# FNet mixing gated by a GLU on one Trainium2 core: a new order table, new page homes, and a first small fetch on ScalarE's queue

## The chip, the cores and the metric

The kernel runs on one core of one Trainium2 chip. The metric is the device time of one execution in microseconds (us), lower being better; the times given are medians over runs. Five engines work side by side, each through its own instructions in the order in which they were issued: TensorE (PE: matmuls; PEld: the loading of their weights), VectorE (DVE), ScalarE (ACT), GpSimd (POOL) and SyncE (SP, which here only issues transfers). Engines wait for each other through semaphores.

## The reference

```python
xn = layernorm(x)                          # x: 2048 x 512
a, b = xn @ dft_hid_re.T, xn @ dft_hid_im.T
s = dft_seq_re @ a - dft_seq_im @ b        # 2048 x 2048 matrices
h = sigmoid(xn @ w_gate) * (xn @ w_up)     # 512 -> 1792
out = x + s * silu(h @ w_down)             # 1792 -> 512
```

All data are float32.

## The kernel before

Matmuls run on pairs of reduced-precision numbers: an operand is split into a high part (`hi`, made by ACT) and the remainder (`lo`, made by DVE), and three matmuls hi·hi, hi·lo, lo·hi are added up (`split`, `mm3`, lines 373 to 380). Large products are cut into 2 x 2 blocks and done with seven block products instead of eight, so DVE also forms sums and differences of blocks ahead of the splits and behind the products.

The work falls into stages. First a head: x is loaded, normalised, transposed by matmuls against an identity matrix, and the first chunks of the gate and up products are taken while matmuls of a tile of ones (`gb`, `ub` from `ones`) keep PE busy. Then seven groups of 256 of the 1792 inner columns, for each half of the sequence: gate and up products from the weights `w_gu`, sigmoid and product, and the down product from `w_down`. Its partial results are added into `g_part` in DRAM by accumulating transfers that POOL issues. The statistics of later rows go through a small DRAM tensor `m_part` and come back broadcast over all partitions; the loaded transposed x (`in_x_t`) is normalised with them by DVE. After that come the sequence transform (blocks of `c_re`, `c_im` loaded, summed by DVE, split; an inner operand kept in `i_part`; sums of xn in `s_part`; results put to `f_part`) and the transform along the hidden axis (`w_h`, `w_part`), with the output added into `out`.

Data live in 54 buffers of the same size in SBUF, called pages (128 partitions x 1024 words, 512 KB); nearly every transfer moves one page. Each new page takes its buffer from the string `HOMES` (lines 270 to 282), letter by letter, so that a letter that comes again is a buffer used again, and the new user waits until the old one's readers are done.

No instruction is issued where the Python code calls it. All calls on the five engines are recorded in a list (`Queue`, `Recorder`, lines 306 to 321), and `emit` (line 324) then issues them by number as the table `ORDER` (lines 33 to 271) lists them. That is why nearly every row of the profile has line 331. The table thus sets the order on each engine and in each queue, and which instruction stands beside which. Lists of due times in the code (such as `LATE3`, `XN`, `CSUM`, lines 645 to 663 and 1040) only set the order of recording.

Loads are issued by SP (`nc.sync.dma_start`), stores and accumulations by POOL (`nc.gpsimd.dma_start`), and a single output piece at the end by ACT. Each queue issues in order: an instruction that waits for its page holds back those behind it.

Of the kernel before, what the change touches and what calls it, by code (L numbers as in the profile page):

```python
# [9 lines left out]
F32 = mybir.dt.float32  # L10
# [5 lines left out]
P = 128  # L16
# [17 lines left out]
1 15 20 0 3 2 4 16 72 5 31 21 7 19 6 22 9 29 11 32 13 23 73 17 8 74 24 10 26 176 25 12 108 27 30 33 50 28  # L34
36-38 211 39 34 40 14 49 51 41 52 48 42 71 43-44 53 70 18 35 55 54 80 56 45 47 46 64 79 65 62 57 63 66 60 81
67-69 59 75-77 82 78 89 84-85 83 86-87 90 88 91 61 92 58 109 96 110 93 101 402 94 97 102 105 98-99 95 100
117-118 113 119-120 103 111-112 104 125-126 154 123 121 124 127 122 128-129 135 130 143 139-140 144-146 106
150 178 151 141 133 155 142 152 114 153 220 230 156 115 157 147-148 443 162 134 163 116 158-159 136 160 164
161 137 180 168-169 177 172-173 206 170 179 138 171 174 201 175 185 165 186 181 191 166 192 149 187-189 218
190 167 203 193-194 212 195-196 182 197 107 198 183 207 204 208 205 199 131 200 221 219 132 222 213 202 214  # L40
231 209-210 223-224 253 242 215-216 225-226 238 217 232 239 227-228 246 243 235 247-248 263 249-250 266 229
236 267 240 284 348 241 285-286 245 233 256-257 287 244 288 254 237 255 258-260 264 261 234 268-269 265
270-271 489 272 251 273-275 293-294 262 276-277 289-290 278 252 279 303 282 304 280-281 361 291 283 292 295
302 296 381 297-298 312-313 301 299 324 300 316-317 320 309 423 321 305 307 306 325 314 340 315 318 310 319
322 362 323 663 330 311 331 349-352 341 444 353 326 354 445 328 344 329 469 332 363 333 470 334-335 327 336
403 337 355-357 345 358 346 359-360 365-366 541 364 367-371 347 377 372-374 379 375-376 442 383-384 378 385
438 386 382 387-389 380 395 390-392 446 393-394 397 424-425 396 426 308 427 399 428 420 429 338 398 436 339
405 404 406 460 407-408 342 409-410 467 411-413 421 414-415 447 416 430-433 417 434-435 439 471 419 472 418
473-474 400 475-476 448 422 483 449-451 437 452-453 440 454 461 455-456 401 464 462 457-459 441 477 465 478
463 479-482 619 491 466 492-493 484 494-495 485 496 343 529-531 545 503 497-498 542 499 468 500-501 487 505  # L50
502 532 535 533 486 534 504 515-516 666 517-518 488 519 536 520 506 552 507 537 553-554 510 590 555-557 580
521-522 527 523-525 511 526 558-561 581 564 562 490 582 563 546 538 547-548 565 549 539 550 592 512 551
566-568 528 569 513 583 570 540 571-572 593-594 575 595-597 573 598 577 599 696 514 600-602 574 603-604 606
584 605 705 608 668 609 543 610 631-632 576 633-634 544 635 607 636 648 585 591 643 649 588 586 650 664 645
614 508 646 184 587 647 625 611 620 612-613 637 578 651 638 621 639 589 615 640-641 669 652 642 616 654-655
617 656-657 653 627 658-659 644 670 626 671 622 661 672-673 660 674-675 618 629 676 662 677-679 682 680 630
681 686 683 687-689 692 684 690-691 685 726 509 693 727 697 728 698 694 729-730 709 731-732 712 623 713 695
628 714-715 733 716 624 717 710 718 699 719 724 700 720-722 707 701 711 723 735-737 970 738 667 665 739-741
706 757 703 758 742 759 773 760 747 761 743 725 762-764 777 765 734 751 708 769 752-754 744 755-756 969 750
797-799 745 771 789 749 790-791 795 792 746 793-794 774 766 815 767 781 768 783 775 778 784-785 770 704 786  # L60
772 787 779 788 748 809-811 776 803 800-802 782 796 806-807 804 808 829 812 830 850 805 831-832 816 780
833-834 823-824 813 825 859 826 821 827 814 828 846 840-841 835 842 817 837 860 838-839 862-863 971 864 836
865 847 866 844 818 848 867-868 843 869 935 870 874 871 845 822 872-873 878 875 879 849 880 930 881 884 882
876 883 887 931 885 888 851 819 889 886 890 893 891 897 892 906 857 852 907 877 908 853 909-910 855 858
911-912 894 913-914 932 915 898 916 978 899 917 904 923 968 924 900 925 856 920 896 921-922 967 936 918 926
937-939 927 919 940-941 929 928 972 951 861 980 952 965 953 948 973 955 949-950 934 902 942 975 954 943-944
905 1093 945 981 946 895 947 956-957 901 999 979 958-959 976 962 960-961 987 966 1022 988-990 977 991-992
963 933 1001-1002 985 1003 1054 1004-1005 982 1006-1007 993-995 1000 996 986 997 1008 998 1010 1026 1011
1009 1012 1021 1013-1014 983 964 1015 1023 1028-1030 1016 1031-1032 984 1033 1017 1034-1035 1024 1036-1037
1027 1040 1038-1039 1042 1041 1043-1044 1052 1045 579 1046-1047 1118 820 1057 1048 1018 1025 1058 854 1059  # L70
1049 1060 1119 1061 702 1053 1062 1073-1074 1157 1050 1075-1076 1079 1077-1078 1063 1080 1064-1066 1055
1067-1068 1082-1083 1069 1084-1085 1070 1086 1071 1087-1088 1096 1158 1097 1089 1098 1072 1099-1100 1165
1090 1056 1101 1111-1113 1108-1109 1122 1110 1124-1126 1120 1127-1128 1094 1129-1130 1136 1131-1133 1115
1121 1134-1135 1114 1102 1095 1103 1116 1104 1081 1105 1091 1106-1107 903 1166 1156 1141-1143 1217 1147-1148
1137 1149 1138 1117 1153 1139-1140 1167 1123 1144 1168-1170 1145 1171-1172 1092 1146 1150-1152 1173 1154
1174-1176 1179 1019 1177-1178 1202-1204 1159 1205 1164 1206-1207 1160 1184-1186 1193 1181 1188 1182 1161
1183 1196 1180 1197 1051 1198 1194 1199-1201 1231 1190 1187 1232-1233 1191 1234 1020 1219 1189 1235-1236
1211-1212 1155 1213 1192 1255 1215 1256-1258 1223 1259 1162 1260 1208 1195 1209 1250 1210 1225 1214 1220
1226-1227 1252 1228 1221 1216 1229-1230 1224 1240-1242 1237 1244 1238 1222 1239 1261 1243 1262-1264 1267
1251 1265-1266 1246 1272 1248 1273 1268 1274 1269 1279 1270-1271 1289 1280 1275 1290-1292 1253 1247  # L80
1293-1294 1283-1284 1276 1285 1278 1286 1218 1287-1288 1299 1277 1296 1300 1249 1301-1302 1281 1305 1303
1245 1304 1319 1295 1254 1320-1321 1311 1322-1324 1297 1313 1306 1314-1315 1282 1307 1316-1317 1298 1318
1325-1326 1312 1327-1328 1331 1329-1330 1354 1334 1355-1356 1338 1335 1357-1359 1308 1340 1332 1341-1342
1423 1343-1345 1360 1346 1163 1352 1347 1361 1348-1349 1339 1350 1363 1362 1351 1387-1389 1353 1333
1379-1381 1366 1382 974 1383-1384 1367 1390 1386 1391-1392 1369 1373 1397 1374-1375 1336 1376 1364 1377-1378
1368 1435 1385 1436-1437 1337 1438 1454 1439 1365 1440 1394 1456 1408-1409 1371 1410 1399 1411-1413 1393
1429 1372 1430 1425 1431 1395 1432-1434 1310 1414 1427 1415-1416 1402-1403 1400 1426 1404-1407 1420 1417
1398 1418 1309 1419 1515 1459-1461 1396 1462 1370 1463 1421 1464 1401 1441 1422 1471 1442-1445 1455 1446
1465 1448 1466 1428 1467-1468 1447 1469-1470 1473 1451 1472 1474-1478 2059 1485 1480 1486 1452 1487-1488
1457 1489-1492 1479 1458 1493-1494 1450 1495 1481 1496-1497 1501 1516 1502 1511 1449 1503 1517-1519 1499  # L90
1520 1482 1521-1522 1498 1484 1504-1505 1538 1506 1523 1507 1524 1483 1525-1527 1453 1528-1529 1566 1530
1508 1531 1500 1542 1509 1543 1597 1544 1513 1545-1546 1540 1547-1548 1541 1549 1554 1550-1552 1567 1553
1565 1556 1539 1557 1571 1558 1602 1532-1535 1559-1560 1596 1536 1561 1573-1574 1563 1555 1537 1575-1576
1562 1577 1568 1578 1590 1564 1585 1591 1514 1592 1579 1594 1580-1582 1604 1512 1583-1584 1587-1589 1510
1608 1593 1609 1569 1610-1611 1424 1595 1612 1603 1613 1633 1600 1634-1636 2060 1637 1586 1638 1620 1572
1631 2061 1621-1624 1598 1629 1625 1570 1639-1640 1601 1641 1626 1642-1644 1627 1614 1658 1615 1606
# [238 lines left out]
def fnet_glu_kernel(ctx: ExitStack, tc: tile.TileContext, x, x_t, c_re, c_im, w_h, w_gu, w_down, out):  # L335
# [1218 lines left out]
```

## Time and profile before

| | |
|---|---|
| median of 3 runs | 802.28 us (800.14 to 802.34) |
| the profiled execution's own time | 807.1 us |
| its span, first to last instruction | 805.3 us |
| mean granted TensorE clock | 0.999 |
| PE busy | 786.8 us (98%), 3488 matmuls |
| DVE busy | 735.6 us (91%) |
| ACT busy | 546.6 us (68%) |
| POOL busy | 132.5 us (16%) |
| moved by transfers | 190.98 MB, 237 GB/s over the span |

Busy time is the union of an engine's instructions. A busy PE need not be a PE at full rate, so the number of matmuls in a stretch says more than its busy time. In the rows of a timeline, the brackets at the end give how long the engine was idle just before, and what it waited for by the profile's inference. A row on SPq or POOLq is the issue of a transfer.

### The profile page before, as it was taken

How to read it: one execution, taken by the hardware profiler on the slowest of the kernel's cores; microseconds unless marked ns; L12 is line 12 of the kernel's file. 1: busy time of each engine (PE TensorE's matmuls, PEld its weight loads, DVE VectorE, ACT ScalarE, POOL GpSimd, SP SyncE). 2: the span in 40 equal slices, each digit the busy share in tenths (PEclk: the TensorE clock that was granted, in tenths of full speed). 3: DMA queues.
4: the chain of work that ended last, by engine and by line, in shares of the span. 5: the costliest groups of instructions: out<-in, count | busy, mean ns of one | idle time of the engine just before them, and what ended most of it. 6: DMA issues, size and time to landing. Idle time of an engine off the chain costs nothing.

```text
span 805.3 us, 10034 instructions
## 1 busy us (share of the span) xinstructions
PE 786.8 (98%) x3488; PEld 642.9 (80%) x3488; DVE 735.6 (91%) x893; ACT 546.6 (68%) x800; POOL 132.5 (16%) x181
## 2 busy tenths in 40 slices
PE   8999999898999999999999999999999999999997
PEld 7888788686788888888888877778778888888885
DVE  8999997788987979899999987899999999999984
ACT  6778999577776878877887944655475264649450
POOL 3004452121122222311201100100100100001031
PEclk9999999999999999999999999999999999999999
DMA  9403999887679999999987899968995986888066
GB/s 343 128 27 131 231 219 208 203 170 157 146 163 282 251 256 277 285 285 214 258 290 273 192 293 320 270 195 316 384 384 199 393 317 224 328 351 313 1 97 112
DMA packets 54786, 190.98 MB, mean 237 GB/s; under 512 B 6096, under 2 KB 6352, under 8 KB 54736
## 3 DMA queue, kind: packets, MB, share of 16 engines
q0 software_dynamic: 21168, 73.42, 41.0%
q1 hardware_dynamic: 33488, 116.87, 39.9%
q8 instruction: 27, 0.44, 0.2%
q14 instruction: 23, 0.19, 0.1%
q10 hardware_dynamic: 80, 0.07, 0.0%
HBM read 120.06 MB, written 73.94 MB: 241 GB/s over the span
## 4 chain that ended last, share of the span: by engine, by line
PE 74%; DMA 11%; issue 6%; DVE 5%; ACT 1%; POOL 1%; SPq 0%; DVEq 0%; ACTq 0%; POOLq 0%
PE pd L331 16%; PE ga L331 11%; PE ua L331 10%; PE gb L331 9%; PE ub L331 9%; PE uc L331 9%; PE gc L331 9%; DVE page L331 5%; DMA g_part<-page 3%; DMA f_part<-page 2%; DMA page<-in_c_re_dram 2%; DMA page<-i_part 2%; DMA page<-in_w_gu_dram 1%; ACT page L331 1%; DMA page<-in_c_im_dram 1%
## 5 line engine op out<-in xcount | busy, mean ns | idle before, releaser
L331 DVE TENSOR_TENSOR page<-page 128x1024 f32<-128x1024 f32 (+5 forms) x712 | 646.6, 970 | 35.3 <-ACT page L331 17.2
L331 ACT ACTIVATE page<-page 128x1024 fp32r<-128x1024 f32 (+4 forms) x392 | 350.6, 935 | 133.5 <-DVE page L331 89.0
L331 PE MATMUL pd<-page 128*128 128x512 f32 x708 | 185.0, 392 | 5.1 <-ACT page L331 3.9
L331 PEld LDWEIGHTS pd<-page 128*128 128x128 f32 x708 | 131.6, 188 | 37.2 <-ACT page L331 8.4
L331 PE MATMUL ga<-page 128*128 128x512 f32 (+1 forms) x558 | 142.0, 387 | 0.5 <-DVE page L331 0.5
L331 PE MATMUL ua<-page 128*128 128x512 f32 (+1 forms) x546 | 140.1, 388 | 1.1 <-DVE page L331 0.6
L331 POOL DMA_DIRECT2D g_part<-page x84 | 70.7, 893 | 322.9 <-ACT page L331 304.8
L331 PEld LDWEIGHTS ga<-page 128*128 128x128 f32 x558 | 103.9, 188 | 22.8 <-issue 0.9
L331 PEld LDWEIGHTS ua<-page 128*128 128x128 f32 x546 | 101.6, 188 | 23.8 <-DVE page L331 2.0
L331 ACT ACTIVATE page<-pd 128x512 f32<-128x512 f32 (+2 forms) x165 | 91.4, 576 | 36.0 <-PE pd L331 30.9
L331 PE MATMUL gc<-page 128*128 128x512 f32 (+1 forms) x420 | 108.7, 384 | 0.3 <-DVE page L331 0.3
L331 PE MATMUL uc<-page 128*128 128x512 f32 (+1 forms) x420 | 107.8, 384 | 0.3 <-DVE page L331 0.3
L331 PE MATMUL gb<-page 128*128 128x512 f32 (+1 forms) x420 | 104.6, 382 | 0.5 <-ACT gb L331 0.5
L331 PE MATMUL ub<-page 128*128 128x512 f32 (+1 forms) x384 | 99.2, 387 | 2.1 <-ACT ub L331 1.8
L331 PEld LDWEIGHTS gc<-page 128*128 128x128 f32 x420 | 77.5, 188 | 17.1 <-DVE page L331 1.6
L331 PEld LDWEIGHTS uc<-page 128*128 128x128 f32 x420 | 77.8, 188 | 16.5 <-DVE page L331 1.0
L331 PEld LDWEIGHTS gb<-page 128*128 128x128 f32 x420 | 76.5, 188 | 17.0 <-ACT gb L331 1.2
L331 PEld LDWEIGHTS ub<-page 128*128 128x128 f32 x384 | 71.4, 188 | 18.0 <-ACT ub L331 2.9
L331 ACT ACTIVATE page<-ga 128x512 f32<-128x512 f32 x48 | 28.6, 597 | 13.5 <-PE ga L331 12.0
L331 POOL DMA_DIRECT2D f_part<-page x16 | 8.7, 543 | 168.0 <-DVE page L331 142.0
L331 DVE TENSOR_TENSOR page<-page,gc 128x512 f32<-128x512 f32 x34 | 23.2, 683 | 8.8 <-PE gc L331 6.6
L331 ACT ACTIVATE page<-ua 128x512 f32<-128x512 f32 x34 | 20.4, 599 | 12.9 <-PE ua L331 11.2
(62 smaller groups left out, 256.4 us busy)
## 6 DMA issues: line engine op xcount, KB each, us to landing
g_part<-page POOLq DMA_DIRECT2D x84, 512.0 KB, 7.5
page<-in_c_re_dram SPq DMA_DIRECT2D x64, 512.0 KB, 6.1
page<-in_c_im_dram SPq DMA_DIRECT2D x33, 512.0 KB, 6.3
page<-i_part SPq DMA_DIRECT2D x28, 512.0 KB, 6.1
page<-in_w_gu_dram SPq DMA_DIRECT2D x24, 512.0 KB, 6.7
f_part<-page POOLq DMA_DIRECT2D x16, 512.0 KB, 6.8
page<-f_part SPq DMA_DIRECT2D x16, 512.0 KB, 6.2
i_part<-page POOLq DMA_DIRECT2D x14, 512.0 KB, 7.5
```

The source lines that it names most:

```text
L331: f(*map(found, a), **{n: found(v) for n, v in k.items()})
```

## The change

The instructions are those of before but for one. The table `ORDER` and the string `HOMES` are replaced by others, made with longer transfers assumed; and right after the identity matrix, ACT's queue fetches 32 words of the first two weight tiles into a tile `touch` that nothing reads. All lines of the code behind the table stand a little further down, so that the recorded instructions show line 332 in place of 331.

```diff
 ORDER = """
-1 15 20 0 3 2 4 16 72 5 31 21 7 19 6 22 9 29 11 32 13 23 73 17 8 74 24 10 26 176 25 12 108 27 30 33 50 28
+1 15 20 0 3 2 16 72 5 31 4 21 7 19 6 22 9 32 11 29 13 176 17 53 74 8 23 33 10 73 24 26 25 108 36 27 30 28
...
 HOMES = (
-    "abcdefghijklmnopqrstuvwxyzABCDEFGHIJKLMNOPQRSTUVWXYZ01ospduyBAFrGJCDTwq1xMdPegAISKNXUvBxDELhqPdxtBwK"
+    "abcdefghijklmnopqrstuvwxyzABCDEFGHIJKLMNOPQRSTUVWXYZ01nupdvCBzFqAJGDTsrY1fMQxezSvPLNIwKXTEhsYy1tTDPS"
...
     ident = const.tile([P, P], F32, name="ident")
     make_identity(tc.nc, ident)
+    touch = const.tile([P // 8, 2], F32, name="touch")
+    tc.nc.scalar.dma_start(touch, w_gu[0, :, :: 8, 0, :1].rearrange("k p o -> p (k o)"))
     ones = const.tile([P, 512], F32R, name="ones")
```

What the tables do is seen in the rows of the engines. The number behind a name is the buffer's, given out in the order of issue, so that the same data bear other numbers in the two kernels.

Place 1 is SP's queue where the second half of the sequence is normalised (between the 530th and the 720th matmul of the program). The rows are loads; `m_part` holds the statistics, `in_x_t` the transposed x that they normalise. Before:

```order
L331 DMA page_1270<-in_x_t_dram 128x1024
L331 DMA page_1283<-in_w_gu_dram 128x1024
L331 DMA page_1380<-in_x_t_dram 128x1024
L331 DMA page_1388<-in_x_t_dram 128x1024
L331 DMA page_1489<-m_part_80 128x1024
L331 DMA page_1542<-m_part_80 128x1024
L331 DMA page_1579<-in_w_gu_dram 128x1024
```

And in the changed kernel:

```order
L332 DMA page_1296<-m_part_82 128x1024
L332 DMA page_1305<-in_x_t_dram 128x1024
L332 DMA page_1353<-in_w_gu_dram 128x1024
L332 DMA page_1360<-in_x_t_dram 128x1024
L332 DMA page_1371<-in_w_gu_dram 128x1024
L332 DMA page_1553<-in_w_gu_dram 128x1024
L332 DMA page_1576<-in_x_t_dram 128x1024
L332 DMA page_1613<-m_part_82 128x1024
```

The first `m_part` load now stands ahead of the three `in_x_t` loads instead of behind them, and the two no longer follow each other. In the table, 23 matmuls stood between the first of them (page_1489) and the DVE instruction that waits for it; now 99 do (page_1296). For the second it was 75 (page_1542), and is 31 (page_1613).

Place 2 is SP's queue in the sequence transform, around the 2170th matmul. The rows are loads of the transform's blocks (`in_c_re`, `in_c_im`) and of the kept inner operand (`i_part`). Before:

```order
L331 DMA page_4584<-in_c_im_dram 128x1024
L331 DMA page_4589<-in_c_re_dram 128x1024
L331 DMA page_4617<-in_c_re_dram 128x1024
L331 DMA page_4625<-in_c_re_dram 128x1024
L331 DMA page_4639<-i_part_91 128x1024
L331 DMA page_4646<-in_c_re_dram 128x1024
```

And in the changed kernel:

```order
L332 DMA page_4632<-in_c_im_dram 128x1024
L332 DMA page_4636<-in_c_re_dram 128x1024
L332 DMA page_4661<-in_c_re_dram 128x1024
L332 DMA page_4674<-i_part_93 128x1024
L332 DMA page_4684<-in_c_re_dram 128x1024
```

Four loads in a row had 18, 21, 18 and 17 matmuls up to the instruction that waits for them (page_4617, 4625, 4639, 4646); the corresponding four now have 23, 19, 18 and 16 (page_4636, 4661, 4674, 4684). Here the order has changed and the distance has not.

Place 3 is POOL's queue around the 840th matmul, where partial results are added into the four `g_part` tensors of the first half; an addition into a tensor waits until the one before it into the same tensor has landed. Before:

```order
L331 DMA g_part2_83<-page_1748 128x1024
L331 DMA g_part0_81<-page_1724 128x1024
L331 TENSOR_SCALAR shifts_79<-moments_77 128x1
L331 DMA g_part3_84<-page_1811 128x1024
L331 DMA g_part1_82<-page_1854 128x1024
L331 DMA g_part2_83<-page_1911 128x1024
```

And in the changed kernel:

```order
L332 DMA g_part1_84<-page_1861 128x1024
L332 DMA g_part2_85<-page_1738 128x1024
L332 DMA g_part3_86<-page_1885 128x1024
L332 DMA g_part2_85<-page_1926 128x1024
L332 DMA g_part0_83<-page_2000 128x1024
```

Between the two additions into the same tensor (`g_part2`) there stood 84 matmuls in the table; now there are 23.

Over the whole program behind the first 80 matmuls, the median number of matmuls between a load of SP and the first instruction of PE, ACT or DVE that waits for it goes from 43 to 52 (204 loads each). Loads with fewer than 27 matmuls go from 43 to 23: from 3 to 0 between the 560th and the 900th matmul, and from 27 to 15 between the 1870th and the 2570th.

More of the change, by code (lines that the diff above doesn't have):

```diff
@@ L264 @@
[L264 to L267 removed]
+1 15 20 0 3 2 16 72 5 31 4 21 7 19 6 22 9 32 11 29 13 176 17 53 74 8 23 33 10 73 24 26 25 108 36 27 30 28
+211 50 37-40 34 12 48 14 51 18 49 41 52 42-43 71 44-45 80 35 70 57 79 64 47 65 54 101 56 62 102 63 81 55 66
@@ new lines @@
+1057 1049 1058 1054 1059-1060 1048 1061 986 1062 1055 1050 1076-1078 1073 1217 974 1074-1075 1063 1079
+1064-1066 1080 1067-1069 1085-1086 1070 1087 1082-1083 1072 1084 1096 1071 1088 1097-1099 1089 1056
+1100-1101 1223 1111-1113 1108-1110 1124 1114 1125-1126 1052 1127 1094 1128-1129 1157 1130 1136 1131 1115
+1132-1133 1423 1051 1134-1135 1141 1091 1142 1090 1143 1095 1120 1150-1152 1156 1102-1103 1053 1116
+1104-1105 1165 1106 1121 1107 1167 1117 1168 1145 1169 1081 1170 1193 1171 1122 1172 1147 1137 1148-1149
@@ new lines @@
+1286-1287 1224 1288 1272 1295 1273-1274 1269 1253 1249 1270-1271 1289 1248 1290 1276 1291-1292 1275
+1293-1294 1297 1302-1304 1299 1306 1300-1301 1254 1313 1296 1314 1277 1315 1311 1316-1317 1281 1318 1328
+1305 1329 1298 1330 1307 1319-1320 1312 1321-1324 1245 1334 1325 1282 1326-1327 1308 1354-1356 1278
+1357-1360 1340-1341 1163 1335 1342 1361 1343-1344 1218 1345 1390 1352 1391 1331 1392 1346 1332 1347-1348
+1363 1349 1333 1350-1351 1387 1353 1388-1389 1338 1379 1366 1380-1382 1369 1383-1384 1373 1367 1386
@@ new lines @@
+1374-1376 1393 1368 1377-1378 1454 1435 1364 1436 1336 1385 1437 1399 1438 1397 1439-1440 1337 1429-1430
+1339 1394 1431-1433 1425 1395 1434 1402 1365 1403 1398 1404 1427 1405-1407 1459 1371 1455 1460-1462 1396
+1463 1400 1464 1310 1414-1418 1456 1419 1408 1309 1421 1409 1372 1410-1411 1420 1412-1413 1515 1422 1444
+1426 1445-1446 1441 1370 1362 1448 1442-1443 1401 1465 1447 1466-1468 1471 1449 1469 1597 1470 1482
+1473-1474 1516 1457 1475 1485-1487 1472 1488 1483 1489-1490 1428 1476-1478 1491 1480 1492 1451 1493-1494
@@ new lines @@
+1479 1495-1497 1501 1566 1502 1498 1503 1540 1517 1424 1452 1518-1520 1450 1521-1522 1499 1523 1538
+1524-1525 1453 1526 1507 1527-1528 1458 1504-1506 1542 1508 1481 1543 1539 1544-1545 1511 1500 1546-1547
+1532 1484 1533 1513 1534 1529-1531 1509 1554 1548-1549 1535 1550 1512 1551 1565 1552-1553 1556 1536 1557
+1541 1558 2060 1559 1537 1560-1561 1510 1573 1563 1574 1555 1575-1576 1562 1577 2059 1578 1564 1590-1591
+1567 1592 1568 1587 1571 1588-1589 1514 1579-1580 1593 1581-1582 1604 1583 1713 1584 1608-1609 1714 1594
@@ new lines @@
+1707-1708 1848 1701 1709 1717 1847 1718 2233 1703 1719 2231 1720 1711 1721 2234 1722 1660 1723 1738
+1724-1726 1686 1727 2232 1728-1729 2235 1730 1687 1731-1732 1735 1733-1734 1757 1736 1758 1818 1759 1754
+1737 1739 1755-1756 2096 1746 1702 1747 1761 1748-1749 2098 1750 1760 1751 2099 1784 1819 1712 1785 1762
+1786 1767 2030 1822 1768 2064 1769 1753 1770-1772 1821 1740 2097 1741 2065 1742 2100 1743-1745 1788 1773
+1820 1752 1774-1775 2196 1776 2062 1777 1763 1778 2063 1812 1939 1813 2066 1814 1764 1781-1783 1765 1803
@@ new lines @@
+1910 2034 2016 1967 2017-2018 2052 2022 2053-2054 2004 1985 2024 2005-2006 2002 2007-2008 1995 2009 2049
+2056 2050 2003 2051 2263 2037-2038 2265 2039 2035 2040 1997 2041 1911 2042 2090 1986 2091 2036 2092 2405
+2043 2055 2044-2045 2331 2475 2046 2094 2047-2048 2103 2087 2473 2088-2089 2204 2010 2093 2011 2474
+2012-2013 2136 2161 2095 2014 2476 2015 2079 2162 2080 2068 2332 2194 2081-2082 1998 2083-2084 2070 2073
+2086 2074-2075 2104 2076 2403 2077 2058 2078 2404 2111 2069 2298 2112 2057 2296 2113-2114 2067 2268
@@ new lines @@
+2115-2116 2477 2264 2121 2118 2122-2124 2120 2127 2125-2126 2144 2085 2406 2269 2145 2367 2146 2128 2407
+2147-2148 2368 2101 2149 2187-2188 2137 2369 2189 2184 2191 2185-2186 2105 2071 2102 2106-2107 2239
+2108-2109 2190 2110 2195 2205 2225 2299 2117 2226 2192 2227 2266 2222 2206 2223-2224 2138-2139 2376 2207
+2140-2143 2176 2119 2159 2177-2179 2370 2160 2180 2168 2181 2208 2072 2209-2210 2229 2211-2212 2228 2213
+2169-2171 2372 2230 2172 2270 2173-2175 2267 2150 2129 2182 2151-2152 2254 2401 2156 2255 2183 2256 2214
@@ new lines @@
+2438 2215 2260 2373 2216-2217 2135 2193 2218-2219 2371 2333 2153-2154 2201 2536 2155 2257 2220 2258 2202
+2259 2248-2249 2297 2237 2250 2203 2300 2251-2253 2304 2240 2307-2309 2238 2310 2335 2311-2312 2261
+2274-2275 2271 2157 2276 2262 2277-2279 2158 2289 2340 2290-2291 2241 2286 2293 2287-2288 2242 2292 2243
+2236 2244-2245 2221 2294 2246-2247 2272 2313-2316 2302 2317 2273 2318 2324 2320 2325-2326 2321 2436 2328
+2322 2334 2323 2402 2348 2327 2349 2437 2350-2351 2305 2341 2329 2352-2353 2361-2362 2355 2374 2363 2280
@@ new lines @@
+2449 2710 2455 2397 2500-2501 2479 2434 2502 2497-2499 2398 2462 2456 2480 2457 2504 2458-2460 2503 2461
+2445 2485 2463 2486-2487 2538 2488 2483 2489 2566 2490 2527-2528 2620 2529 2547 2478 2531 2548-2549 2484
+2550 2539 2551-2552 2518-2519 2510 2567 2520-2524 2511 2525-2526 2541 2530 2542-2543 2653 2544 2554 2545
+2534 2546 2508 2491-2494 2553 2495-2496 2509 2558-2560 2555 2562 2556 2537 2557 2512 2561 2513 2683
+2514-2516 2540 2517 2568 2533 2569-2571 2769 2563 2944 2572-2573 2535 2584 2580 2585 2532 2586 2621
@@ new lines @@
+2865-2869 2980 2870 2888 2930 2872 2931-2932 2950 2946 2936 2951-2953 2889 3112 2954-2955 2933-2934 2914
+2935 3039 2956-2958 2937 2959-2960 2915 2961 2938 2924 2963 2982 2925-2927 2939 2884 2928-2929 2916 2989
+2890 2912 2990-2992 2962 2993-2994 2947 2983 2996 2984-2985 2948 2998 2986-2988 2917 3009 2964 2975
+2965-2966 3046 2970 3047 2949 3048-3049 2995 3050-3051 2967 2997 2968 3066 2969 2981 2971 3090 2972
+3002-3003 2940 3004 2976 2999-3001 2942 3067 3010-3012 3053 3013-3014 3126 3123 3015 3040-3042 3005 3043
@@ new lines @@
+3259-3260 3239 3262 3261 3263-3265 3270 3240 3266-3267 3280-3281 3251 3282 3134 3293 3171 3294-3295 3032
+3277 3172 3299 3278-3279 3271 3286 3310 3287 3062 3288 3392 3283-3284 3274 3285 3030 3296-3298 3311 3303
+3306 3312 3348 3313-3316 3215 3300 3320-3321 3483 3323 3322 3301 3338-3340 3317 3302 3318 3336 3319
+3324-3326 3393 3327 3307 3328-3329 3341-3342 3364 3268 3343 3333-3334 3308 3335 3362 3330-3332 3350 3481
+3289 3351-3352 3356 3291 3357-3358 3337 3353-3354 3345 3355 3359 3504 3360 3363 3361 3366-3367 2973
@@ new lines @@
+3449 3478 3523 3489 3450-3451 3494 3462 3495-3496 3482 3491 3479 3492 3604 3493 3490 3500 3480 3501-3502
+3511-3512 3484 3513 3497 3487 3498-3499 3517 3522 3518 3456 3488 3519 3508 3506 3509-3510 3528 3486
+3529-3530 3514 3520 3515-3516 3525 3503 3526-3527 3537 3521 3531 3538 3532-3533 3540-3541 3573 3542 3602
+3546-3548 3648 3534 3507 3535-3536 3543 3558 3544-3545 3552 3549-3551 3685 3560 3553 3561 3603 3562 3566
+3539 3567 3554 3568 3563-3565 3555 3569-3571 3556 3578-3579 3559 3557 3580 3574 3581-3584 3607 3575
@@ new lines @@
+3854 3812 3941 3813-3814 3849-3851 4037 3809-3811 3815-3816 3793 3817 3820 3802 3821-3822 3855 3835 3856
+3844 3857 3823 3803 3824-3825 3897 3859-3864 3898 3865 3869-3871 3866 3845 3924 3867-3868 3829 3967
+3830-3831 3873 3884 3833 3885-3886 3826 3914 3827 4026 3828 3887-3888 3832 3889 3874 3984 3875 3843
+3876-3878 3925 3879 3932 3965 3955 3933-3934 3968 3893-3895 3915 3929-3930 3882 3931 3890-3891 4011 3892
+3935 4055 3936-3938 4002 4203 3939-3940 3881 3942-3944 3883 3899-3901 3945-3946 3969 3947 3902-3904 3908
@@ new lines @@
+4640 4645-4646 4678 4647 4651 4609 4652-4653 4664 4648-4650 4641 4666 4663 4667-4668 4693 4669-4670 4665
+4671 4675-4676 4608 4677 4672 4610 4718 4673-4674 4698-4699 4473 4700 4689 4683 4738 4684-4685 4313
+4686-4687 4682 4688 4709 4695-4697 4704 4722 4760 4705-4706 4777 4701-4703 4694 4711 4900 4712 4802
+4713-4715 4710 4716 4723-4724 4680 4725-4726 4761 4727 4737 4728 5036 4729-4732 4736 4740 4776 4741-4742
+4733-4734 4739 4735 4752 4746-4748 4743 4762 4717 4744-4745 4749 4940 4750 4832 4751 4764 5115 4765-4766
@@ new lines @@
+5032 4963 5478 4970 4975 5219 4976-4977 5148 5084 4978 5038 4979 5035 4980-4981 5070 4982-4983 4974
+4992-4993 5000 4994-4996 5003 4997 5004-5006 4984 5001 4985-4986 5361 5007-5008 5198 5009 4991 5010 5215
+5011-5012 5039-5040 5048 5041-5044 5013 5068 5309 5014-5015 5151 5017-5018 5086 5019 5052 5081 5023-5025
+5053 5079 5054 5071 5055 5020-5022 5029 5059 5045 5060-5061 5033 5026-5028 5072-5073 5082 5074-5077 5087
+5030 5088-5092 5111 5056-5058 5097-5098 4971 5099-5101 5095 5102-5106 5093 5107-5108 5062 5080 5094
```

411 lines of the change are left out of this document (168 added, 243 removed).

## The prediction

> **What bounds the kernel now.** I read the page's head first, then the stretches of the span, the groups and issues of transfers, and then the timeline at the places where matmuls are missing.
>
> ```profile
> span 805.3 us, 10034 instructions
> PE 786.8 (98%) x3488; PEld 642.9 (80%) x3488; DVE 735.6 (91%) x893; ACT 546.6 (68%) x800; POOL 132.5 (16%) x181
> ```
>
> PE is the bound, and the change leaves its 3488 matmuls as they are. What can change is the time in which it gets none. The stretches show that; in each row the first number is the length, the number in brackets behind an engine its instructions:
>
> ```profile
> 80.00:140.00 60.00, 59.88 (x262) 48.66 (x261) 54.19 (x84) 54.81 (x88) 24.20 (x29) 1.00 0.99 220
> 140.00:215.00 75.00, 70.22 (x299) 54.75 (x298) 64.00 (x82) 54.00 (x86) 14.58 (x18) 1.00 0.78 162
> 215.00:300.00 85.00, 84.95 (x374) 69.54 (x373) 71.05 (x115) 64.64 (x116) 21.98 (x32) 1.00 0.92 241
> 300.00:440.00 140.00, 140.00 (x618) 115.28 (x617) 134.34 (x174) 112.42 (x172) 22.70 (x30) 1.00 0.96 268
> 440.00:500.00 60.00, 58.80 (x256) 47.43 (x255) 54.66 (x53) 38.76 (x50) 7.46 (x10) 1.00 0.93 262
> 500.00:600.00 100.00, 96.64 (x418) 77.45 (x417) 93.99 (x88) 57.87 (x69) 8.85 (x13) 1.00 0.89 307
> 600.00:720.00 120.00, 120.00 (x530) 99.01 (x529) 117.26 (x110) 65.62 (x74) 4.83 (x9) 1.00 0.82 312
> ```
>
> In 300:440 PE has no idle time: 140 us / 618 = 0.2265 us a matmul, and 120 / 530 gives the same. At that rate 299 matmuls need 67.7 us, so 140:215 loses 7.3 us. In the same way 500:600 loses 100 - 94.7 = 5.3, 440:500 loses 60 - 58.0 = 2.0, 80:140 loses 0.7 and 215:300 loses 0.3. Together 15.6 us of the 805.3 are lost to waits. That is all that a better order can win behind the head.
>
> Two places carry it: A, 140:215 (7.3 us), and B, 440:600 (7.3 us). What waits at A is in the timeline there:
>
> ```profile
> 140.67 2.13 SPq L331 DMA_DIRECT2D page<-m_part  x2
> ...
> 148.94 11.24 DVE L331 TENSOR_TENSOR page<-page 128x1024 f32<-128x1024 f32 x13 [4.88 <-DMA page<-m_part]
> ...
> 152.73 1.06 ACT L331 ACTIVATE page<-page 128x1024 fp32r<-128x1024 f32 x1 [3.88 <-DVE page L331]
> ...
> 154.32 0.96 PE L331 MATMUL pd<-page 128*128 128x512 f32 x3 [1.16 <-ACT page L331]
> ```
>
> The load of the statistics is issued at 140.67, DVE needs it 4.88 us before it lands, ACT then waits for DVE and PE for ACT: one late transfer passed on through three engines. At B it is the same with another load, its transfer first, from the chain that ended last:
>
> ```profile
> 496.32 6.28 DMA page<-in_c_re_dram
> ```
>
> ```profile
> 502.76 2.00 ACT L331 ACTIVATE page<-page 128x1024 fp32r<-128x1024 f32 x2 [5.64 <-DMA page<-in_c_re_dram]
> ...
> 503.85 3.50 DVE L331 TENSOR_TENSOR page<-page 128x1024 fp32r<-128x1024 f32 x3 [2.49 <-ACT page L331]
> ...
> 504.67 0.58 ACT L331 ACTIVATE ub<-gb 128x512 f32<-128x512 f32 x1
> ...
> 505.30 1.66 PE L331 MATMUL ub<-page 128*128 128x512 f32 x6 [1.58 <-ACT ub L331]
> ```
>
> ACT stands still for 5.64 us until the block has landed, and PE's next sum is started by an ACT copy queued behind it. How long transfers take, in us from issue to landing at the end of each row:
>
> ```profile
> g_part<-page POOLq DMA_DIRECT2D x84, 512.0 KB, 7.5
> page<-in_c_re_dram SPq DMA_DIRECT2D x64, 512.0 KB, 6.1
> page<-i_part SPq DMA_DIRECT2D x28, 512.0 KB, 6.1
> page<-m_part SPq DMA_DIRECT2D x3, 512.0 KB, 8.2
> ```
>
> A load takes 6.1 us, as long as 27 matmuls (27 x 0.2265 = 6.12).
>
> **The change part by part.** The sum is made on the profiled execution: span 805.3 us, own time 807.1.
>
> *Place A.* The first statistics load had 23 matmuls (5.2 us) up to the DVE instruction that waits for it, against a landing of 8.2; it now has 99 (22.4 us), and the second 31 (7.0 us). Loads with a lead under 27 matmuls fall from 3 to none there. So this wait goes, and with it DVE's late start, which feeds ACT and PE. What is late next is POOL: two additions into g_part2 now stand 23 matmuls apart (5.2 us), and the second has to wait for the first, 7.5 us by the row above. That is 2.3 us in which POOL holds what is queued behind it, the additions into g_part0 and g_part2 and with them the pages that ACT writes next. The longest such wait so far:
>
> ```profile
> POOL g_part L331 <- DMA g_part<-page: 10.6, 2, 6.1
> ```
>
> So it costs PE between nothing (the next user of that page has room) and 6.1 us; I take the 2.3. The second statistics load, 7.0 against 8.2, may keep DVE waiting 1.2 us; DVE is idle for 11 of the 75 us there, which covers it. Place A: 7.3 - 2.3 = 5.0 us won; bounds 1.2 and 7.3.
>
> *Place B.* Short leads fall from 27 to 15 of the loads there. I let the loss shrink in that proportion: 7.3 x 15/27 = 4.1 us stay, 3.2 us are won. It is not less because the worst run of loads is not eased: around the 2170th matmul four loads in a row have 23, 19, 18 and 16 matmuls where 18, 21, 18 and 17 stood, 3.6 to 5.2 us against 6.1. DVE has no room to take up such delays: in both tables 78 instructions on a whole page and 10 on half a page stand between the 2140th and the 2570th matmul, by the groups and the timeline
>
> ```profile
> L331 DVE TENSOR_TENSOR page<-page,gc 128x512 f32<-128x512 f32 x34 | 23.2, 683 | 8.8 <-PE gc L331 6.6
> ```
>
> ```profile
> 569.33 6.90 DVE L331 TENSOR_TENSOR page<-page 128x1024 f32<-128x1024 f32 x6
> ```
>
> 78 x 1.15 + 10 x 0.68 = 96.5 of the 97.4 us that 430 matmuls take. Whatever DVE waits there beyond 0.9 us, PE waits. Bounds: nothing won, and all 7.3.
>
> *Elsewhere behind the head* 1.0 us is lost (0.7 and 0.3). The median lead of a load grows from 43 to 52 matmuls, 2.0 us more; I take half, 0.5 won, between 0 and 1.0. The transfers in 215:440 hide behind PE now; what it costs if that ends is the second rival.
>
> *The small fetch* is issued by ACT ahead of the sigmoid table's load. An issue on ACT's queue took 0.57 us at the end of this execution:
>
> ```profile
> 800.46 0.57 ACTq L331 DMA_DIRECT2D out_dram<-page  x1
> ```
>
> The start of the kernel, from the timeline:
>
> ```profile
> 0.73 1.35 SPq L331 DMA_DIRECT2D page<-in_x_dram  x3
> ...
> 2.02 0.20 ACT L331 ACTIVATE warm<-mhalf 128x1 f32<-128x1 f32 x1
> 2.12 0.43 SPq L331 DMA_DIRECT2D page<-in_w_gu_dram  x1
> ...
> 3.53 0.69 DVE L331 BATCH_NORM_STATS2 stats<-page 128x6 f32<-128x512 f32 x1 [2.09 <-DMA page<-in_x_dram]
> ...
> 6.18 0.69 DVE L331 BATCH_NORM_STATS2 stats<-page 128x6 f32<-128x512 f32 x1 [0.41 <-DMA page<-in_x_dram]
> ...
> 6.52 0.66 ACT L331 ACTIVATE page<-pd 128x256 fp32r<-128x256 f32 x2 [4.30 <-PE pd L331]
> ...
> 7.38 0.66 PE L331 MATMUL pd<-ident,page 128*128 128x128 f32 x4 [0.66 <-DVE page L331]
> ...
> 8.13 0.63 ACT L331 ACTIVATE page<-page 128x512 fp32r<-128x512 f32 x1 [0.95 <-DMA page<-in_w_gu_dram]
> ...
> 9.09 0.50 PE L331 MATMUL ua<-page 128*128 128x256 f32 x2 [0.46 <-ACT page L331]
> ```
>
> ACT is idle from 2.22 to 6.52, so the issue is covered. The first weights take from 2.12 to 8.1, 6.0 us, the first x only 0.73 to 3.5, 2.8 us; a fetch of words from the same tensor ahead of them may shorten the first access. But even if they came 3.2 us earlier, the transposes of the second x tile end at 8.04, and its copy and the split of the weights still follow on ACT. Only DVE's 0.41 us of waiting for x would go. I take 0.3 us won; at worst the words hold x up by the 3.2 us that the weights are slower, which would be lost in full. The tail is the same twelve half-width matmuls and four DVE steps in both, so nothing is won there.
>
> *Sum:* 5.0 + 3.2 + 0.5 + 0.3 = 9.0 us. The profiled execution would take 798.1 instead of 807.1. The median of the runs, 802.28, is 4.8 us below the profiled one. If that is a fixed extra, 9.0 carry over whole: 793.3. If it is waits that the other runs do not have, 10.8 of 15.6 are there to win from, and 9.0 x 10.8/15.6 = 6.2 give 796.1. I take 794.5, between them.
>
> **The rivals.**
>
> *The leads do not count (no change, 802.3).* A load's place in SP's queue is not its issue: SP mostly waits until a page is free.
>
> ```profile
> SPq L331 <- DVE page L331: 308.6, 67, 56.0
> ```
>
> If pages come free no earlier than before, the loads go out when they did, the waits stay, and the median stays at 802.3. Against it: the statistics load at A now stands 22.4 us ahead of its user, with its own page given anew. For it: at B, the four loads named above. The DMA page of the Trainium skill (DMA: Bandwidth & Descriptors, Anatomy of one DMA) leads to the same result by another way: its fit for transfers of the software queue, 2.0 us plus bytes / 436e3, makes 3.2 us of a 512 KB page by my estimate, and then leads of 16 matmuls (3.6 us) were enough already and the waits had other causes. The trace disagrees: 7.5 us is the median of 84 such transfers.
>
> *Transfers lengthen as they go out earlier (slower, 806.5).* In 215:440 the transfer engines are 0.92 to 0.96 busy, and PE loses 0.3 us of 225. Loads that go out 2.0 us earlier meet more of POOL's writes. If the writes' landing grows from 7.5 to over 9.5 us, the longer leads are eaten up, A and B keep their loss, and 215:300 begins to wait as 140:215 does: 7.3/75 of 85 us is 8.3, and half of it, since only the additions are late, 4.2. For it: these shares. Against it: the bytes are the same, and 140:215, with the least busy transfers (0.78), loses most, so it was not the load on the engines that made them late there.
>
> **How the numbers follow.** A measurement of this kernel can tell about 0.3%, 2.4 us, from no change. The forecast case, some gain at A and B, runs from 788 (all waits gone: 802.3 - 10.8 = 791.5, or 802.3 - 15.9 = 786.4 if the profiled execution had no extra waits) to 799.9, and I give it 0.68. No change, 799.9 to 804.7: 0.15. Slower: 0.17. The range is 788 to 804.5, with little left out below and most of the slower case above. The chances of faster, same and slower are these three.
>
> **What would show it right or wrong.** Right: in the stretch that holds matmuls 560 to 900 (140:215 before) DVE no longer waits for m_part, and 299 matmuls take about 70 us; at matmul 2170, a wait of ACT, DVE or PE for in_c_re or i_part is still there, 1 to 3 us. POOL's wait for g_part stands near the 866th matmul with 2 to 6 us. The first product starts between 8.7 and 9.1 us. Wrong: A still loses 5 us or more; or g_part's landing is over 9.5 us; or new gaps appear in what was 215:440; or the first product starts after 10 us.

## The result and the profile after

The changed kernel takes 797.9 us (median of 5 runs, 796.5 to 798.3), the kernel before beside it 801.6 (5 runs, 800.1 to 802.3). The ratio is 0.995, with a 95% interval of 0.9935 to 0.9965: faster by 0.5%, 3.7 us. With 12 and 35 runs on another chip it was 0.9947 (0.9926 to 0.9967). Predicted were 794.5, in a range from 788 to 804.5.

The profiled execution of the changed kernel took 796.5 us (span 794.2). First the chain of work that ended last; before, 11% of it was DMA and 6% issue:

```profile
PE 94%; DVE 5%; issue 1%; ACT 0%; DVEq 0%; ACTq 0%
```

Then the windows that the prediction spoke of (busy time and number of instructions of PE, PEld, DVE, ACT, POOL; granted clock; transfer share; GB/s):

```profile
140.00:215.00 75.00, 74.83 (x330) 61.15 (x329) 70.92 (x92) 60.00 (x94) 17.18 (x20) 1.00 0.90 184
...
300.00:440.00 140.00, 139.44 (x611) 113.71 (x611) 128.19 (x157) 108.98 (x162) 22.07 (x27) 1.00 0.93 255
440.00:500.00 60.00, 59.61 (x262) 48.74 (x261) 55.33 (x54) 40.32 (x53) 4.40 (x7) 1.00 0.88 273
500.00:600.00 100.00, 99.78 (x435) 80.74 (x435) 98.65 (x92) 58.34 (x70) 8.03 (x12) 1.00 0.87 298
```

Read the count behind PE's busy time. At 0.2265 us a matmul, place A (140:215) holds 330 matmuls where 299 stood, and loses 75 - 330 x 0.2265 = 0.3 us instead of 7.3. Place B (440:600) holds 697 where 674 stood, and loses 2.1 instead of 7.3. The stretch 300:440 lost nothing and now loses 1.6. With 0.2, 1.0 and 0 in 80:140, 215:300 and 600:720, that is 5.2 us in all where 15.6 were lost.

What is left of the waits for transfers, over the whole run (us in total, times, the longest):

```profile
POOL g_part L332 <- DMA g_part<-page: 9.5, 4, 7.2
...
ACT page L332 <- DMA page<-w_part: 3.3, 1, 3.3
...
ACT page L332 <- DMA page<-in_c_re_dram: 0.9, 1, 0.9
```

DVE's wait for m_part (4.9 us) is gone, ACT's waits for in_c_re (10.1 us over the run, 7.6 of them between 440 and 600) shrank to 0.9, and POOL's waits for its own additions remain. The transfers themselves hardly changed; from issue to landing:

```profile
g_part<-page POOLq DMA_DIRECT2D x84, 512.0 KB, 7.2
page<-in_c_re_dram SPq DMA_DIRECT2D x64, 512.0 KB, 5.5
```

### The profile page after: what moved, and what is told of

Read it like the earlier page. It is cut to its first block, busy times and chain, and to the rows that moved or that the text cites. A ratio compares the mean times of both kernels' runs of the same rounds, so it can differ in the third digit from the quotient of the medians.

```text
span 794.2 us, 10072 instructions
## 1 busy us (share of the span) xinstructions
PE 785.4 (99%) x3488; PEld 643.5 (81%) x3488; DVE 736.1 (93%) x893; ACT 546.5 (69%) x800; POOL 134.4 (17%) x181
## 4 chain that ended last, share of the span: by engine, by line
PE 94%; DVE 5%; issue 1%; ACT 0%; DVEq 0%; ACTq 0%
PE pd L332 20%; PE ga L332 15%; PE ua L332 15%; PE uc L332 11%; PE gc L332 11%; PE ub L332 11%; PE gb L332 10%; DVE page L332 5%; ACT page L332 0%; DVE ones L332 0%; DVEq L332 0%; ACTq L332 0%
## 5 line engine op out<-in xcount | busy, mean ns | idle before, releaser
L332 DVE TENSOR_TENSOR page<-page 128x1024 fp32r<-128x1024 f32 (+5 forms) x712 | 646.5, 970 | 24.8 <-ACT page L332 15.8
L332 DVE TENSOR_TENSOR page<-page,uc 128x512 f32<-128x512 f32 x36 | 24.6, 682 | 11.1 <-ACT page L332 6.1
```

The lines of the kernel that those rows point to most:

```text
L332: f(*map(found, a), **{n: found(v) for n, v in k.items()})
```

## The experiments

The theory: the gain is that of leads. A wait goes when a transfer's page is free, and the transfer issued, early enough to land before its user. The rivals: the new order of the engines' own work; the choice of the homes as such; the small fetch.

### The kernel before, profiled again

> The kernel before, unchanged, profiled a second time. If the 4.8 us by which its profiled execution lay over the median were waits of that one execution, this profile shows a shorter span (about 796 to 801 us) and less than 15.6 us lost behind the head, with the same places named, and the shrunken places tell which waits come and go. If they are a fixed extra of profiling, the span is 805 again with 15 to 16 us lost, 7.3 of them in 140:215 and 7.3 in 440:600.

It took 805.8 us (span 804.1). Its windows and its wait for the statistics:

```profile
140.00:215.00 75.00, 73.21 (x317) 58.38 (x316) 68.05 (x87) 57.34 (x89) 15.30 (x19) 1.00 0.86 177
...
440.00:500.00 60.00, 58.76 (x257) 47.57 (x256) 53.38 (x51) 36.93 (x47) 5.85 (x8) 1.00 0.90 266
500.00:600.00 100.00, 95.32 (x412) 76.28 (x411) 94.20 (x88) 58.54 (x70) 8.87 (x13) 1.00 0.91 308
```

```profile
DVE page L331 <- DMA page<-m_part: 3.8, 2, 3.4
```

The places stay, the sizes do not: A loses 3.2 here and lost 7.3, B loses 8.5 and lost 7.3. By what was expected beforehand this decides nothing: the span of 804.1 and 14.7 us lost in all speak for a fixed extra, A's 3.2 speaks for waits that come and go. More is seen across the kernels. The three profiled executions of this order with its own homes were all long ones: 807.1, 805.8 and, with the small fetch, 806.4, each 4 to 5 us over the median of the same kernel's runs. Six profiled executions in the changed order, those whose homes fit it, lay between 1.4 us under and 2.3 us over their medians, and the order of before with place A mended (next section) 1.0 over. So the extra on which the prediction hesitated is not the same for every kernel; it goes where the waits go. Why a profiled execution of before meets the larger waits each time is not shown.

### Place A alone

```diff
 ORDER = """   (before)
-... 889 886 890 ... 1120 1127-1128 1094 ... 1119 1061 702 1053 ... 1106-1107 903 1166 ...
+... 889 886 702 890 ... 1120 1127 903 1128 1094 ... 1119 1061 1053 ... 1106-1107 1166 ...
```

Number 702 is POOL's write of the first statistics, 903 SP's load of them. In `HOMES`, the letters R and 1 change places from that load on.

> Place A alone, without disturbing other pages: in the kernel before, POOL's write of the first statistics stands some 70 matmuls earlier and SP's load of them 24 entries earlier, and homes R and 1 change names from that load on, so that by the profile of before its page is free at 136.0 us (the load went out at 140.67, when the write had landed), while the one displaced page waits 0.1 us. Theory 1 (the wait for the landing): DVE's wait for m_part, 3.4 to 5.8 us in three profiles, falls to 0 to 1.1; 140:215 loses 0 to 3 us instead of 3.2 to 7.3; the median is 1.5 to 4 us under the kernel before, and the spread of its runs stays, since 500:600 still loses 5 to 7. Rival (the wait only moves: DVE then waits for pages that POOL's additions still read, 2.4 to 4.1 us there before): DVE's or ACT's wait for g_part grows by what m_part's falls, median within 1 us of before.

The ratio to before is 0.996 (0.9939 to 0.998), 798.8 against 801.3 us: 2.4 us for two entries and one exchange of names, where the changed kernel beside it on the same chip has 3.2. The intervals of the two overlap, so that by their times place A alone cannot be told from the whole change. The load went out at 132.9 instead of 140.7 us, by the row of SP's queue, and no wait for m_part is left. That row, and the windows:

```profile
132.88 9.05 SPq L322 DMA_DIRECT2D page<-m_part  x2
```

```profile
140.00:215.00 75.00, 75.00 (x332) 61.87 (x331) 71.75 (x91) 59.66 (x94) 15.62 (x20) 1.00 0.83 175
...
440.00:500.00 60.00, 57.80 (x250) 46.29 (x249) 52.28 (x50) 37.09 (x48) 5.13 (x7) 1.00 0.90 275
500.00:600.00 100.00, 96.66 (x420) 77.92 (x420) 95.97 (x90) 57.52 (x68) 7.98 (x12) 1.00 0.90 310
```

Place A loses nothing, place B its 8.2 us as ever, with ACT waiting for the same loads:

```profile
ACT page L322 <- DMA page<-in_c_re_dram: 10.3, 4, 4.9
```

What held the load in before stands in SP's waits between 110 and 165 us. It was not the page, whose last reader had ended at 138.9 us:

```profile
SPq L331 <- DMA m_part<-moments: 12.4, 1, 12.4
```

SP waited 12.4 us for POOL's write of the statistics, which had gone out at 126.9 us and landed at 140.5. In the changed kernel that write goes out at 107.8 us, and in this run at 108.6. The rows of POOL in before and in the changed kernel:

```profile
126.89 1.70 POOL L331 DMA_DIRECT2D m_part<-moments  x1
```

```profile
107.82 1.09 POOL L332 DMA_DIRECT2D m_part<-moments  x1
```

So place A is mended first of all in POOL's queue, which the lists of SP's loads do not show. Write and load were moved together here, so what each would win alone is not known.

So the late statistics carried all that A lost in the profile: with them early, PE's gaps near 183 and 200 us went too, where the trace of before names ACT and pages held by g_part. DVE's wait for pages that POOL's additions still read did not grow either (5.8 us in before, 1.2 here). That settles A, and since the engines' own order is otherwise that of before, the rival of a new order of their work falls for A. For B no such single load was taken alone; that its gain comes from leads rests on the waits for in_c_re that went, not on an experiment. The times of the runs do not show that gain either, since the kernel that still loses 8.2 us at B in its profile cannot be told from the changed one.

### The order with other homes

Four kernels keep an order and change only `HOMES`; each new page gets a place by a rule: the place free longest, or the one freed last, counted by instructions in the order table, or (the fourth) by times. A fifth was a first try at place A, with 702 and 903 moved and 28 other homes changed to make room.

```diff
-HOMES = ("abcdefghijklmnopqrstuvwxyzABCDEFGHIJKLMNOPQRSTUVWXYZ01nupdvCBzFqAJGDTsrY1f..."   (changed kernel)
+HOMES = ("01ABCDEFGHIJKLMNOPQRSTUVWXLYZSNabcdeBfTgZYhXiaLbeOjaSkQlmnopqrPkDTCrhiVjYgd..."   (freed last)
```

> The order of before, with other page homes: each new page takes the place that has been free longest. That takes away some of the short leads: added over the loads behind the head, what a lead from the page's last reader to the new page's first reader lacks to 32 matmuls is 178 matmuls before and 126 here (49 in the changed kernel). Theory 1 (leads): about (178-126)/(178-49) = 0.4 of the gain of the changed kernel, 1 to 2 us faster than before. Theory 3 (order of the work): no change, within 1 us. If the homes of the changed kernel are what counts: 3 to 4 us faster.

> The order of the changed kernel, each new page in the place that has been free longest: the lack to 32 matmuls is 41 instead of 49, so theory 1 says 0 to 0.5 us faster than the changed kernel (797 to 798 us, ratio to before 0.994 to 0.996); theory 3 says the same time.

> The order of the changed kernel, with other page homes: each new page takes the place that came free last. Leads get short again: what they lack to 32 matmuls adds up to 209 behind the head (178 in before, 49 in the changed kernel); the order of every engine's work stays that of the changed kernel. Theory 1 (leads): the gain is gone, 801 to 806 us, with DVE, ACT or PE waiting for loads in 300:440 (lack 43, 4 there in the changed kernel) and in 500:600 (92, was 32), and little lost in 140:215 (3). Theory 3 (order of the work): the gain stays, 797 to 799 us.

> Place A alone: the kernel before with two entries of its order moved, POOL's write of the first statistics to DRAM (about 40 matmuls earlier) and SP's load of them (its page now free 149 matmuls ahead of its first reader instead of 28), and its page home with 28 later homes shifted by a rank to make room. Theory 1 (the wait for that load is what place A loses): 140:215 loses 0 to 2.5 instead of 7.3, 440:600 loses 7.3 as before, the time is 3 to 5 us under the kernel before. Theory 2 (several loads with short leads each cost their own part of A): only the gaps around 150 to 160 go, 2.5 to 3 us, the ones around 174 to 205 stay. Theory 3 (leads do not count, what counts is the new order of DVE and ACT): 140:215 still loses about 7, time unchanged within 1 us.

| kernel | us | ratio to before |
|---|---|---|
| order of before, free longest by the table | 947.2 | 1.184 (1.178 to 1.190) |
| changed order, free longest by the table | 966.6 | 1.205 (1.202 to 1.209) |
| changed order, freed last by the table | 1226.8 | 1.529 (1.525 to 1.534) |
| first try at A, 28 homes shifted | 841.0 | 1.050 (1.046 to 1.054) |
| changed order, by times | 799.9 | 0.997 (0.995 to 1.000) |

All four expectations that counted by the table were wrong, by 40 to 420 us. ACT and DVE wait for a transfer that still reads the page they are to write. In before, in its order with places free longest, in the changed order with places freed last:

```profile
DVE page L331 <- DMA g_part<-page: 5.8, 4, 2.7
ACT page L331 <- DMA g_part<-page: 2.3, 3, 1.4
```

```profile
ACT page L331 <- DMA g_part<-page: 82.8, 29, 8.3
...
DVE page L331 <- DMA g_part<-page: 54.0, 17, 6.0
```

```profile
ACT page L332 <- DMA g_part<-page: 154.0, 28, 12.7
DVE page L332 <- DMA g_part<-page: 128.4, 22, 13.7
```

The table counts such a page as free where POOL's addition is listed; in truth it is free when the addition has landed, 7.2 us after its issue, and the issue itself may stand in POOL's queue. Set against the times of the changed kernel's profile, with 9 us for a transfer that reads a page, 32 of its 834 first writes of a page by ACT or DVE come before that page is surely free, 29 of them because of a transfer of POOL. With places free longest by the table it would be 124, 110 of them because of POOL; with places freed last 416, but only 112 because of POOL. There 300 come before an instruction of PE, DVE or ACT is done with the page, so the landing of transfers is only a part of what freed-last costs. The fourth kernel was made from these times to test this, with 30 such writes:

> The order of the changed kernel with page homes chosen anew by the times of its own profile, a page read by a DMA counted as taken until 9 us behind its issue: a load takes the place free longest, a write of ACT or DVE the one freed last before its time. Theory 4 (the homes must know the landing of POOL's writes, and that alone is why the two earlier sets of homes, chosen by the order alone, cost 168 and 429 us): within 3 us of the changed kernel, 795 to 801, ratio to before 0.990 to 0.998, with ACT's waits for g_part's DMA below 10 us in all (83 us with the first of those sets). If something else in the set of homes matters (which place it is, and not when it is free): 20 us slower or more.

```profile
DVE page L332 <- DMA g_part<-page: 2.4, 2, 1.8
ACT page L332 <- DMA g_part<-page: 1.2, 1, 1.2
```

799.9 us: of the 169 us that the first set cost, 167 are back, with the same order and wholly other places. Up to 2 us, which place a page has does not matter; when it is free does. The 1.9 us that are left against the changed kernel beside it (798.0) were not explained. It also means that the order by itself wins nothing here: with places free longest it takes 966.6 us where the order of before takes 947.2, and it has its gain only with homes that fit its times.

### The head and the small fetch

The small fetch alone in the kernel before, the changed kernel without it (on two chips), and the changed kernel with the three matmuls of ones (12, 14, 18) behind the second transposes:

```diff
 ORDER = """   (changed)
-... 39-40 34 12 48 14 51 18 49 41 52 42-43 71 44-45 ...
+... 39-40 34 48 51 49 41 52 42-43 71 44 12 14 18 45 ...
```

> The kernel before with only the small fetch of weights added on ACT's queue. By the head of the changed kernel, the third tile of x should no longer be waited for and its statistics start at about 5.5 instead of 6.2 us, and the split of the weights should not wait for them. If that frees the head, the first product starts 0.3 to 0.6 us earlier than 9.09, and the time falls by as much, under what the runs can tell; if the copy of the second x tile and the order on ACT hold it, it starts at 9.0 to 9.1. If the small fetch has a cost of its own, the first x tile's statistics start later than 3.53.

> The changed kernel without the small fetch. If the small fetch is what makes the slow first accesses to the weights milder, the third x tile is waited for again (its statistics start at about 6.2 instead of 5.5 us) and the first w load lands later; the first product then starts at 9.0 to 9.6 us, the time rises by 0 to 0.6 us, which the runs can hardly tell. The ratio to before is 0.995 to 0.997. If the small fetch does more, the gain over before shrinks by over 1 us.

> The changed kernel without the small fetch once more, now on the same chip as the changed kernel itself. If the small fetch costs something, this is 1 to 2 us faster than the changed kernel beside it (796.2 against 797.9 on two chips); if the difference was that of the chips, they agree within 0.7 us. The start of the first product has ranged from 8.07 to 9.46 us in ten profiles, five with and five without the fetch, so nothing is expected of its place in one profile.

> The changed kernel with the three matmuls of ones that stand ahead of the transposes of the second x tile moved behind them. If these three are what kept the earlier x from showing, the second transposes start at 6.7 to 6.9 us instead of 7.42, the split of the weights at 7.6 to 7.9 instead of 8.34 and the first product at 8.3 to 8.6 instead of 9.01, and the whole is 0.4 to 0.7 us shorter. If the weights or ACT hold the first product, it stays at 8.9 to 9.0.

Before with the fetch: 801.3 us, 0.9992 (0.9961 to 1.0023). The changed kernel without it: 796.2, 0.9917 (0.9897 to 0.9937), and on the other chip 797.3 with 798.0 for the changed kernel beside it, both 0.9947 of before. With the ones moved: 797.2, 0.9931 (0.9912 to 0.995), on the chip of the 796.2, where the changed kernel itself was not run. So neither edit can be told from nothing. The first product in the profiles of before with the fetch, of the changed kernel without it, and of the changed kernel with the ones moved:

```profile
8.07 0.51 PE L331 MATMUL ua<-page 128*128 128x256 f32 x2
```

```profile
8.29 0.51 PE L332 MATMUL ua<-page 128*128 128x256 f32 x2 [0.99 <-ACT page L332]
```

```profile
6.57 0.69 DVE L323 BATCH_NORM_STATS2 stats<-page 128x6 f32<-128x512 f32 x1 [0.95 <-DMA page<-in_x_dram]
...
9.41 0.51 PE L323 MATMUL ua<-page 128*128 128x256 f32 x2 [0.41 <-ACT page L323]
```

In the last, the third x tile came late although the fetch was there. In the fourteen profiles of all kernels the first product starts between 8.07 and 10.29 us, on the mean at 8.92 without the fetch (seven) and at 9.05 with it (seven). What the first loads take differs more from run to run than this edit could change.

### The changed kernel again

> The changed kernel unchanged, on the same chip as the three others of this call: 796 to 799 us, and a spread of its runs under 2.5 us where those of the kernel before spread over 5 to 11. If the spread of before is the lottery of its short leads, before's fastest runs come near this kernel's and its slowest lie 8 us above.

798.0 us, 12 runs from 796.1 to 800.3: a spread of 4.3 us, where under 2.5 was expected. The 35 runs of before lay from 798.0 to 808.0. With place A alone mended they lay from 795.2 to 800.4. On a third chip, where the changed kernel was not run, 17 runs of before ranged from 795.4 to 806.6. A quarter of before's 35 runs lay under 800.0 us and a quarter over 803.8; in the changed kernel these bounds are 796.5 and 798.5. So the whole range moved down, the long runs (5.3 us) more than the short ones (3.4 us).

## Why the prediction was right, step by step

*Place A, 5.0 us won.* That DVE's wait for the statistics carries the loss was right, shown by the run with place A alone mended. What made the load late is not in the prediction: it speaks of its lead in SP's queue and of its page, and SP waited for POOL's write of the statistics. The size was too small: 7.0 us between the profiles. The term that failed is the 2.3 us for POOL's two additions to g_part2. At that place POOL waited for ACT and not for the first addition, which had landed half a us earlier, at 195.1, and its longest wait for an addition stands elsewhere, near the 635th matmul. The second row here is the second addition to g_part2:

```profile
137.70 0.89 POOL L332 DMA_DIRECT2D g_part<-page  x1 [7.19 <-DMA g_part<-page]
```

```profile
195.64 0.86 POOL L332 DMA_DIRECT2D g_part<-page  x1 [8.54 <-ACT ub L332]
```

Even 7.2 us there cost PE nothing that the window shows (80:140 loses 0.2, A 0.3): the low bound, "the next user of that page has room", was the right one.

*Place B, 3.2 us won.* In the profile 5.2 us were, so 2.1 are left, not 4.1. The share of short leads (15 of 27) was no measure of the wait, and no wait of 1 to 3 us was found at matmul 2170: there the longest wait for a transfer is DVE's 0.7 us for in_c_im. The step that failed is setting the four loads in a row against the four that stand in their place in the changed queue: they are in part other loads. The one for which ACT waited 5.6 us in before (page_4617) was issued at 496.3 us and its reader was ready at 502.76 - 5.64 = 497.1, 0.8 us later. In the changed kernel the same instruction (page_4560) went out at the 2125th matmul instead of the 2167th, at 480.2 us, 8.6 ahead of its reader, which then waited 1.1 us for PE and not for it. In both kernels it went out within 0.1 us after the last user of its page had ended. In the two timelines (the row of before holds three loads, of which this is the second):

```profile
490.47 6.89 SPq L331 DMA_DIRECT2D page<-in_c_re_dram  x3
```

```profile
480.20 0.33 SPq L332 DMA_DIRECT2D page<-in_c_re_dram  x1
...
488.81 2.01 ACT L332 ACTIVATE page<-page 128x1024 fp32r<-128x1024 f32 x2 [1.12 <-PE uc L332]
```

*Elsewhere, 0.5 us won.* Instead 1.8 us were lost: 300:440 loses 1.6 where it lost nothing, 215:300 loses 1.0 and not 0.3, and only 80:140 gained, from 0.7 to 0.2. The 1.6 comes again in a second profile of this kernel (610 matmuls, 1.8 us), and its largest gap, 0.45 us, is PE waiting for DVE:

```profile
412.34 1.43 PE L332 MATMUL ub<-page 128*128 128x512 f32 x5 [0.45 <-DVE page L332]
```

It may come with the new order of DVE's work; that was not tried alone. The rival of lengthening transfers is refuted: 7.2 us instead of 7.5, where it asked for over 9.5.

*The small fetch, 0.3 us.* Nothing that can be measured, as above. In the profile of the changed kernel the first product starts at 9.01, inside the forecast 8.7 to 9.1, but a place that wanders over 2.2 us confirms nothing.

*The sum and the carrying over.* The profiled execution was to take 798.1 and took 796.5; 10.4 us of PE's waits went where 9.0 were forecast. That these are so near is in part luck: A and B each won 2.0 more than forecast, and elsewhere came out 2.3 worse. The median fell by 3.7 us and not by 7.8. The step that failed is the carrying over, the middle between "fixed extra" and "waits". Kernels without the long waits hardly have such an extra, so the branch of waits is the nearer one; it gave 796.1. It is still 1.8 low, since it shrinks the gain as if each wait shrank alike. The runs say otherwise: A alone is worth 7.3 us between two profiles and 2.4 between two medians, and how much of B's 5.2 us is in an ordinary run stays open.

*The rival that leads do not count* fell with place A, though it was right that a load's place in SP's queue is not its issue: the write of the statistics set the issue there. In the trace of before the statistics load was issued at 140.7 and its reader was ready at 148.94 - 4.88 = 144.1, 3.4 us later. It landed 8.2 us after its issue, DVE waited 4.9, and issued 7.8 us earlier the wait was gone. By the Trainium skill (DMA: Bandwidth & Descriptors, Anatomy of one DMA), whose fit is for transfers that GpSimd issues, a 512 KB page would take 3.2 us, my estimate. POOL's 84 additions took 7.5 us here, so the measurement decides. The loads go through SP's queue, for which that fit is not stated, so it could not have told whether their leads were enough.

## What to carry to other kernels

Judge a load's lead by the time from the moment when it can go out to its first user, and not by how far ahead it stands in the program. It can go out when the buffer it fills is released and, where it fetches what the kernel itself wrote to DRAM, that write has landed; here the write was what came late. And count a buffer that a transfer reads as taken until the landing. When reordering, choose buffers and order together: here the same order with other buffers took between 2 and 429 us longer. When a profiled execution lies over the median, do not carry its waits over whole: here 10.4 us fewer waits in the profile were 3.7 us in the median.

## What the runs showed that was not expected

Reusing buffers by a rule that knows only the order of the table cost 18 to 53% with identical instructions in identical order, and the granted clock fell with it, to 0.96, 0.95 and 0.87 instead of 1.0 in those profiles. One late 512 KB load of two vectors of statistics, waited for 3.4 to 5.8 us by DVE, cost PE 3 to 7 us over the next 70 us, more than the wait itself in one of the profiles. And on one chip the run-to-run spread was smaller with fewer waits: 2.4 us standard deviation in the kernel before (35 runs), 1.7 with place A mended, 1.4 in the changed kernel (12 each); so few runs hardly tell 1.7 from either.
